# Backward of a spectral and dense block: where w2's gradient is scaled, and when the last stage's inputs are loaded

## The chip, the cores and the metric

One core of a Trainium2 chip runs the kernel in one launch. The metric is device time in microseconds of an execution, as the median of a set of runs. Engines are named PE (matmul), DVE (VectorE), ACT (ScalarE), POOL (GpSimd); the SP queue issues most DMAs.

## The reference

A block with six modulation rows, forward and all gradients but that of `B_x`:

```python
mod = (silu(c) @ w_mod).reshape(1, 6, 1, 512)
sa, ca, ga, sb, cb, gb = ...                       # its six rows
h = layernorm(x) * (1 + ca) + sa
x = x + ga * irfft2(rfft2(h) * (w_r + 1j * w_i))   # 2048 x 512
h = layernorm(x) * (1 + cb) + sb
x = x + gb * (relu(h @ w1 + b1) ** 2 @ w2 + b2)    # inner width 1792
out, vjp = jax.vjp(f, A_x, A_w_r, A_w_i, B_w1, B_b1, B_w2, B_b2, c, w_mod)
return out, *vjp(grad_out)
```

For what follows, three gradients matter. With g the output gradient (2048 x 512) and h the squared relu (2048 x 1792), w2's is h^T (g * gb), b2's is the column sum of g * gb, and that of `A_x` comes out of the last stage, the backward of the spectral mix and of the first layernorm.

## The kernel before, in words

Rows are kept as 16 tiles of 128 (NT = 16), inner features as 14 chunks of 128 (NFC = 14). All arrays are bf16, sums are fp32 in PSUM. The program is written with a tile framework: each tile comes from a named pool with a number of buffers, the framework adds the waits, and each engine and the SP queue then work through a fixed order. That order is chosen when the kernel is built, by program order (raised by `high_priority`) among what is ready. `tc.issue_after(ins)` puts what is traced inside it behind `ins` on that engine or queue. Pools lie on a stack on either side of SBUF, so a new pool may have to wait until the work on an old one's tiles has ended.

The parts up to some 290 us (forward, dense backward, the forward half of the spectral backward) are untouched. After them come:

1. `spec_f23` with `ew_b` and `after_b` (eight groups gi). For each group PE does the transforms L323 and L311, ACT copies out, DVE does the complex products (`cmul`, L418 to L421), which give Z in place and gW, the filter gradients; SP writes gW out (L1170; three buffers). `after_b` runs after each group: it loads later groups, puts in units of w1's gradient (`fill_w1`, L1126, 16 units of 16 matmuls, copied by ACT L1130, written out by POOL L1132), takes the products for the modulation rows (`gm.emit`: broadcast L463, copy L465, DVE L474 and L475, ACT L472, output by POOL L477), loads the transform LGb (L1177), the first two `hn` (h's chunk, transposed by DMA from `h_dram`, L1067) and at group 5 the whole output gradient `g_sb` (L1188, 2 MB).
2. `spec_g1` (L346, eight groups of two halves in four PSUM buffers). The halves are copied to CS in turn by DVE (L351) and ACT (L353); psF follows with L365 and L367.
3. The last stage, eight pairs of row tiles. `g2_pair` makes psT (L375) and ACT copies it to Tsb (L377); `row_pair` makes psY (L385), ACT copies it to gs (L1276), DVE unfolds it (L266 to L270), multiplies (L1278), ACT scales with a sum (L1280), then DVE has q1 (L1281, needs n1), jk (L1285), rr, gn, gs and gx (L1287 to L1292), and SP writes gx (L1293). n1 and gxl of a pair come from `load_rows3` (L1222, L1223, pool `fin` with two buffers, two pairs ahead). Column sums go to PE later (L1262).

Between these, `fill` puts in the three last units of w1's gradient and then the 14 units of `grad_w2` (L1203, 16 matmuls each, two PSUM buffers `mm`, copied by DVE with the multiplication by the gate row, L1206, written by SP, L1207). `grad_b2` (L1214, `add_quadrants`) comes once, and two more `gm.emit` at the end; the last instructions are the row for c's gradient, L1319 to L1326.

`load_hn` takes two buffers in `hnp`, then two in `gwp`, and from the point at which w1's gradient is complete four in a pool `endp`; up to four further loads (`endp["more"]`) are put in with the first units.

Of the kernel before, what the change touches and what calls it, by code (L numbers as in the profile page):

```python
# [18 lines left out]
D = 512  # L19
# [4 lines left out]
NT = 16  # L24
# [311 lines left out]
def spec_g1(tc, K, Z, CS):  # L336
    nc = tc.nc
    with tc.tile_pool(name="psG", bufs=4, space=PSUM) as psG_pool, tc.tile_pool(name="psF", bufs=1, space=PSUM) as psF_pool:
        psF = psF_pool.tile([P, 4, P], FP32, name="psF")
        for gi in range(8):  # L340
            for hh in range(2):
# [8 lines left out]
                if hh == 0:  # L350
                    nc.vector.tensor_copy(out=dst, in_=src)  # L351
                else:
                    nc.scalar.copy(out=dst, in_=src)  # L353

            if gi % 2 == 1:
                for ri in range(2):
                    for n in range(2 * gi - 2, 2 * gi + 2):
                        q = 32 * (n % 4)
                        nc.tensor.matmul(psF[q:q + 1, n // 4, :], lhsT=Z[n // 2][:, n % 2, ri, 256:257], rhs=K["LG"][:, n, ri + 1, :],
                                         start=(ri == 0), stop=(ri == 1), tile_position=(0, q))  # L360
        for i in range(4):
# [82 lines left out]
class GMod:  # L444
# [13 lines left out]
    def emit(self, jc, q, row, pool, ppool):  # L458
# [8 lines left out]
        for dc in range(0, 4, 2):  # L467
            wmc = self.tiles[jc][dc // 2]
            gwm = pool.tile([P, 2, D], BF16, name="gwm", bufs=2)
# [11 lines left out]
def kernel(  # L481
# [580 lines left out]
    def load_hn():  # L1062
        fc = len(hns)
        if fc < NFC:
            pool = hnp if fc < 2 else endp.get("hn", endp["gw"])
            hns.append(pool.tile([P, NT, P], BF16, name="hn", bufs=2 if pool is not endp.get("hn") else 4))
            nc.sync.dma_start(hns[fc], h_dram[fc, :, :], transpose=True)  # L1067

    lf2 = tc.alloc_tile_pool(name="lf2", bufs=1, side="right")
    gmp = tc.alloc_tile_pool(name="gmp", bufs=1, side="right")  # L1070
# [22 lines left out]
    def add_quadrants(ps, pool, out, scale=None):  # L1093
# [6 lines left out]
        def add():  # L1100
# [5 lines left out]
            if scale is not None:  # L1106
                nc.vector.tensor_tensor(row, row, scale, op=ALU.mult)
# [6 lines left out]
    def run_later(n=1):  # L1114
        if later:
            later[0][0] -= n
            if later[0][0] <= 0:
                later.pop(0)[1]()

# [29 lines left out]
    with tc.tile_pool(name="f23b", bufs=2) as fr, tc.tile_pool(name="ewb", bufs=2) as ew:  # L1149
# [22 lines left out]
        def after_b(gi):  # L1172
            if gi + 4 < 8:
                load(gi + 4)
            if gi == 3:
                with tc.issue_after(K["gW"]):
                    nc.sync.dma_start(K["LG"], LG_dram)  # L1177
            fill_w1(2 if 0 < gi < 6 else 1)
            if gi == 4:
                with tc.issue_after(K["gW"]):  # L1180
                    load_hn()
                    load_hn()
            if gi == 5:
# [3 lines left out]
                with tc.issue_after(K["gW"]):  # L1187
                    K["g_load"] = nc.sync.dma_start(endp["g_sb"], g_view).ins  # L1188
            if gi in (0, 1, 3, 4):
                gms.pop(0)[1]()  # L1190
                if len(gms) > 1:
                    gm.load(gms[1][0], gmp)
# [3 lines left out]
    fin = tc.alloc_tile_pool(name="fin", bufs=2, side="right")  # L1196
# [3 lines left out]
    def grad_w2(fc):  # L1200
        ps = mmps.tile([P, SB], FP32, name="mm")
# [3 lines left out]
        with tc.high_priority():  # L1205
            nc.vector.tensor_tensor(gw, ps, modb[:, GB_B, :], op=ALU.mult)  # L1206
        nc.sync.dma_start(out6_view[:, fc, :], gw)  # L1207
        load_hn()

    def grad_b2():  # L1210
# [4 lines left out]
        add_quadrants(ps, gwp, out_7[None, :], modb[0:1, GB_B, :])  # L1215

    rows3 = {}

    def load_rows3(t):
        if t < NT:  # L1220
            rows3[t] = (fin.tile([P, 2, D], BF16, name="n1"), fin.tile([P, 2, D], BF16, name="gxl"))
            nc.sync.dma_start(rows3[t][0], n1_dram[:, t:t + 2, :])  # L1222
            nc.sync.dma_start(rows3[t][1], gx1_dram[:, t:t + 2, :])  # L1223

    with tc.issue_after(K["g_load"]):
        load_rows3(0)
        load_rows3(2)
    for _ in range(2):
        load_hn()

    CS = utcs.tile([P, NT, 4, 16, 8], BF16, name="utcs")
    spec_g1(tc, K, Z, CS)
    sp.release()
    lg2.release()
    fp = tc.alloc_tile_pool(name="fin2", bufs=2, side="right")
    psX = tc.alloc_tile_pool(name="psX", bufs=1, space=PSUM)
    units2 = [lambda fc=fc: grad_w2(fc) for fc in range(NFC)]

    def fill(n):
        for _ in range(n):  # L1240
            if units:
                fill_w1(1)
                if not units:
# [3 lines left out]
                    endp["more"] = 4  # L1247
            elif units2:
                units2.pop(0)()
                run_later()  # L1250
                if endp.get("more", 0) > 0:
                    endp["more"] -= 1
                    load_hn()

    with tc.tile_pool(name="psE", bufs=2, space=PSUM) as psE, tc.tile_pool(name="psS1", bufs=1, space=PSUM) as psS1:
# [11 lines left out]
        def row_pair(t, Ts):  # L1267
# [26 lines left out]
            load_rows3(t + 4)  # L1294

        Ts = g2_pair(0)
        for t in range(0, NT, 2):
# [4 lines left out]
            if t == 10:  # L1302
                grad_b2()
        fill(1)
# [6 lines left out]
        for j in range(2):  # L1311
            gm.load(j, endp["gm"])
            gm.emit(j, 32 * j, acc1_sb[32 * j:32 * j + 1, :], endp["gm"], psX)
# [15 lines left out]
    gwp.release()  # L1329
    fin.release()  # L1330
    endp["g"].release()
# [40 lines left out]
```

## Time and profile before

| what | value |
|---|---|
| median of 10 runs | 431.06 us (430.0 to 555.48) |
| the profiled execution | 430.68 us |
| its span in the profile | 428.9 us |
| its mean granted PE clock | 0.996 |
| SP issues in the span: transposing loads of hn | 14, 2.0 to 5.7 us each on the queue, 4.5 to 6.7 us to landing |

The page gives the busy time of each engine over the span, and tables by window cut it into stages. A busy PE need not be PE at its peak. The time reported by the runs contains 1.8 us that lie outside the span.

### The profile page before, as it was taken

Reading aid. Unit: us, or ns where it says so; the run is one execution under the profiler, and the core shown is the slowest. Engines: PE = TensorE matmul, PEld = TensorE weight load, DVE = VectorE, ACT = ScalarE, POOL = GpSimd, SP = SyncE. Lnnn points to the kernel's source line nnn. Section 1 sums busy time; section 2 is a strip of 40 time slices with the busy share of each in tenths; the row PEclk is TensorE's granted clock in tenths of the full one; section 3 lists DMA queues with packets and bytes.
Section 4 is the critical chain, followed back from the end, with each engine's and each line's share of the span. In section 5 each row is a group of like instructions: output and inputs, shape, how many; then the busy total and the mean of one; then the engine's idle time right before and its main releaser. Section 6 shows DMA issues by size and latency. Waiting matters only on the chain.

```text
span 428.9 us, 7116 instructions
## 1 busy us (share of the span) xinstructions
PE 397.6 (93%) x2353; PEld 196.1 (46%) x2375; DVE 354.1 (83%) x862; ACT 256.2 (60%) x487; POOL 54.7 (13%) x135
## 2 busy tenths in 40 slices
PE   2789999999899999999999999999999999898995
PEld 0344446654434444444444444455555654343332
DVE  6799868959996588978897998937998945999994
ACT  5578699778882188248635855454756463536331
POOL 8347940000000000000000000002221000000011
PEclk9999999999999999999999999999999999999899
DMA  8999899969497469767965998988899999999993
GB/s 235 215 263 300 261 213 320 305 222 227 139 357 231 129 93 337 204 168 180 307 168 172 178 318 266 299 171 286 276 250 331 181 248 220 224 247 268 254 255 112
DMA packets 144227, 101.11 MB, mean 236 GB/s; under 512 B 98969, under 2 KB 127518, under 8 KB 143806
## 3 DMA queue, kind: packets, MB, share of 16 engines
q1 hardware_dynamic: 141034, 93.03, 83.3%
q0 software_dynamic: 2592, 7.09, 5.6%
q10 hardware_dynamic: 564, 0.53, 0.5%
q8 instruction: 19, 0.31, 0.3%
q14 instruction: 18, 0.15, 0.1%
HBM read 35.44 MB, written 41.60 MB: 180 GB/s over the span
## 4 chain that ended last, share of the span: by engine, by line
PE 50%; DVE 21%; ACT 15%; DMA 7%; issue 4%; POOL 1%; ACTq 0%; DVEq 0%; SPq 0%
PE og L906 12%; PE mm L877 10%; PE mm L1126 8%; PE mm L712 5%; PE mm L1203 3%; PE psG L346 2%; DMA out_dram<-gW 2%; ACT gab L717 2%; PE psC L311 2%; DVE jk L1285 2%; ACT AE L329 2%; DMA n<-n_dram 2%; DMA wmc<-in_w_mod_dram 1%; PE psB L323 1%; ACT AE L330 1%
## 5 line engine op out<-in xcount | busy, mean ns | idle before, releaser
L712 PE MATMUL mm<-gT,w2T 128*128 128x512 bf16 x224 | 57.8, 383 | 2.9 <-ACT gab L717 2.9
L877 PE MATMUL mm<-h2T,w 128*128 128x512 bf16 x224 | 53.4, 378 | 1.6 <-ACT r L879 1.4
L1203 PE MATMUL mm<-g_sb,hn 128*128 128x512 bf16 x217 | 51.7, 387 | 3.2 <-DVE gw L1206 2.6
L906 PE MATMUL og<-w1T,gab 128*128 128x512 bf16 x218 | 49.9, 379 | 1.0 <-DVE o L971 0.8
L1126 PE MATMUL mm<-gab,h_sb 128*128 128x448 bf16 x256 | 50.7, 352 | 0.0
L906 PE MATMUL og<-w,h 128*128 128x512 bf16 x217 | 49.1, 379 | 0.3
L879 ACT ACTIVATE r<-mm,b1col 128x512 bf16<-128x512 f32 x56 | 37.0, 685 | 6.1 <-PE mm L877 3.3
L1203 PEld LDWEIGHTS <-hn 128*128 128x128 bf16 x224 | 21.6, 100 | 30.0 <-issue 7.7
L877 PEld LDWEIGHTS <-w 128*128 128x128 bf16 x224 | 21.1, 97 | 30.0 <-issue 8.3
L1126 PEld LDWEIGHTS <-h_sb 128*128 128x128 bf16 x256 | 24.6, 98 | 21.8 <-issue 0.6
L906 PEld LDWEIGHTS <-h 128*128 128x128 bf16 x224 | 21.8, 98 | 26.1 <-issue 0.9
L906 PEld LDWEIGHTS <-gab 128*128 128x128 bf16 x224 | 21.6, 98 | 25.9 <-issue 1.4
L712 PEld LDWEIGHTS <-w2T 128*128 128x128 bf16 x224 | 21.2, 98 | 22.4 <-issue 6.3
L1280 ACT ACTIVATE gs<-gn,inv 128x512 bf16<-128x512 bf16 x16 | 11.4, 715 | 25.1 <-DVE gn L1278 25.1
L919 ACT CAST G<-og 128x512 bf16<-128x512 f32 x16 | 9.2, 580 | 28.1 <-PE og L906 28.1
L295 POOL MEMSET AE<- 128x2 bf16 x4 | 0.3, 102 | 194.2 <-DMA gx_dram<-n2rows 194.2
L477 POOL DMA_DIRECT2D out_dram<-gwm x12 | 8.7, 729 | 122.4 <-DMA hn<-h_dram 57.9
L881 DVE TENSOR_TENSOR h<-r 128x1024 bf16<-128x1024 bf16 x28 | 19.2, 685 | 4.8 <-ACT r L879 4.8
L717 ACT CAST gab<-mm 128x512 bf16<-128x512 f32 x36 | 21.3, 600 | 2.0 <-PE mm L712 1.8
L475 DVE SCALAR_TENSOR_TENSOR gm_junk<-wmc,onef,gmbc 128x512 bf16<-128x512 bf16 x24 | 17.9, 745 | 3.0 <-DMA wmc<-in_w_mod_dram 2.0
L715 DVE CAST gab<-mm 128x512 bf16<-128x512 f32 x20 | 13.8, 688 | 7.9 <-PE mm L712 7.7
L377 ACT ACTIVATE Tsb<-psT 128x512 bf16<-128x512 f32 x32 | 18.4, 607 | 1.6 <-PE psT L375 1.5
(290 smaller groups left out, 800.2 us busy)
## 6 DMA issues: line engine op xcount, KB each, us to landing
h_dram<-h SPq DMA_DIRECT2D x28, 256.0 KB, 3.2
gh_dram<-gab SPq DMA_DIRECT2D x28, 256.0 KB, 4.1
w<-in_B_w_dram SPq DMA_DIRECT2D x2, 1792.0 KB
wmc<-in_w_mod_dram SPq DMA_DIRECT2D x12, 256.0 KB, 5.7
out_dram<-gwm POOLq DMA_DIRECT2D x12, 256.0 KB, 6.4
wz_dram<-Z SPq DMA_DIRECT2D x8, 258.0 KB, 3.9
xs_dram<-Xs SPq DMA_DIRECT2D x8, 258.0 KB, 4.3
Z<-wz_dram SPq DMA_DIRECT2D x8, 258.0 KB, 5.5
```

The costliest lines, as they stand in the source:

```text
L377: nc.scalar.activation(Tsb, ps, AF.Copy, scale=EF_S)
L475: nc.vector.scalar_tensor_tensor(out=junk, in0=wmc[:, i, :], scalar=K["onef"], in1=gmbc, op0=ALU.mult, op1=ALU.mult, accum_out=self.gsc[:, ...
L712: nc.tensor.matmul(ps, lhsT=w2T[:, dc, fc * P:(fc + 1) * P], rhs=gT[b][:, :, dc, :], start=(dc == 0), stop=(dc == 3))
L715: nc.vector.tensor_copy(out=gaT[b][:, fc, :], in_=ps)
L717: nc.scalar.copy(out=gaT[b][:, fc, :], in_=ps)
L877: nc.tensor.matmul(ps, lhsT=w1[:, dc, (fc + i) * P:(fc + i + 1) * P], rhs=h2T[b][:, :, dc, :], start=(dc == 0), stop=(dc == 3))
L879: nc.scalar.activation(r[:, i, :], ps, AF.Relu, bias=b1col[:, fc + i:fc + i + 1])
L881: nc.vector.tensor_tensor(h2, r, r, op=ALU.mult)
L906: nc.tensor.matmul(ps, lhsT=lhs(fc), rhs=rhs[:, fc, :], start=(fc == 0), stop=(fc == NFC - 1))
L1126: nc.tensor.matmul(ps[:, 0:W4], lhsT=h2_sb[:, t, dc * P:(dc + 1) * P], rhs=ghn[t // 4][:, t % 4, fs], start=(t == 0), stop=(t == NT - 1))
L1203: nc.tensor.matmul(ps, lhsT=hns[fc][:, t, :], rhs=g_sb[:, t, :], start=(t == 0), stop=(t == NT - 1))
L1280: nc.scalar.activation(gs[:, i, :], gn[:, i, :], AF.Copy, scale=inv1[:, t + i:t + i + 1], accum_out=rr[:, i, 0:1])
```

## The change

- `grad_w2`'s copy out of PSUM is a plain copy by ACT; the gate row is multiplied into `g_sb` in SBUF before, in four DVE instructions of four row tiles each (`scale_g`, called from `spec_g1` after groups 4 to 7, each behind the DVE cast just issued). `grad_b2` then needs no scaling of its own.
- `fin` is allocated earlier, and `load_rows3(0)` and `(2)` follow LGb's load at group 3. Every third pair's rows have a buffer in `fp` (fin2), so loads run three pairs ahead.
- `g_sb` is loaded at group 4, in four pieces, after that group's `gm.emit`; the first two `hn` are issued behind it.
- `load_hn` is issued once at the start of each unit but the first, behind the row load named by `K["rows"]` or the one before it (`K["rows0"]`); the extra loads fall away.
- The last two `gm.load` are issued at t = 10, and the last `gm.emit` has four `gwm` buffers.

```diff
-def spec_g1(tc, K, Z, CS):
+def spec_g1(tc, K, Z, CS, after=None):
...
                 if hh == 0:
-                    nc.vector.tensor_copy(out=dst, in_=src)
+                    K["cast"] = nc.vector.tensor_copy(out=dst, in_=src).ins
...
+            if after:
+                after(gi)
...
-    def emit(self, jc, q, row, pool, ppool):
+    def emit(self, jc, q, row, pool, ppool, nbuf=2):
...
-            gwm = pool.tile([P, 2, D], BF16, name="gwm", bufs=2)
+            gwm = pool.tile([P, 2, D], BF16, name="gwm", bufs=nbuf)
...
-            nc.sync.dma_start(hns[fc], h_dram[fc, :, :], transpose=True)
+            with tc.issue_after(K["rows" if fc < 4 else "rows0"]):
+                nc.sync.dma_start(hns[fc], h_dram[fc, :, :], transpose=True)
...
+    fin = tc.alloc_tile_pool(name="fin", bufs=2, side="right")
     gmp = tc.alloc_tile_pool(name="gmp", bufs=1, side="right")
...
-            if scale is not None:
-                nc.vector.tensor_tensor(row, row, scale, op=ALU.mult)
...
+    def load_rows3(t):
+        if t < NT:
+            pool, n = (endp["fp"], 1) if t % 6 == 4 else (fin, 2)
+            rows3[t] = [pool.tile([P, 2, D], BF16, name=x, bufs=n) for x in ("n1", "gxl")]
+            nc.sync.dma_start(rows3[t][0], n1_dram[:, t:t + 2, :])
+            K["rows0"] = K.get("rows")
+            K["rows"] = nc.sync.dma_start(rows3[t][1], gx1_dram[:, t:t + 2, :]).ins
...
             if gi == 3:
                 with tc.issue_after(K["gW"]):
                     nc.sync.dma_start(K["LG"], LG_dram)
+                    load_rows3(0)
+                    load_rows3(2)
             fill_w1(2 if 0 < gi < 6 else 1)
+            if gi in (0, 1, 3, 4):
+                gms.pop(0)[1]()
+                if len(gms) > 1:
+                    gm.load(gms[1][0], gmp)
             if gi == 4:
-                with tc.issue_after(K["gW"]):
-                    load_hn()
-                    load_hn()
-            if gi == 5:
                 gmp.release()
...
                 with tc.issue_after(K["gW"]):
-                    K["g_load"] = nc.sync.dma_start(endp["g_sb"], g_view).ins
-            if gi in (0, 1, 3, 4):
-                gms.pop(0)[1]()
-                if len(gms) > 1:
-                    gm.load(gms[1][0], gmp)
+                    for t in range(0, NT, 4):
+                        K["g_load"] = nc.sync.dma_start(endp["g_sb"][:, t:t + 4, :], g_view[:, t:t + 4, :]).ins
+                with tc.issue_after(K["g_load"]):
+                    load_hn()
+                    load_hn()
...
     def grad_w2(fc):
+        if fc > 0:
+            load_hn()
...
-            nc.vector.tensor_tensor(gw, ps, modb[:, GB_B, :], op=ALU.mult)
+            nc.scalar.copy(out=gw, in_=ps)
         nc.sync.dma_start(out6_view[:, fc, :], gw)
-        load_hn()
...
-    with tc.issue_after(K["g_load"]):
-        load_rows3(0)
-        load_rows3(2)
-    for _ in range(2):
-        load_hn()
...
+    def scale_g(gi):
+        if gi >= 4:
+            gs = g_sb[:, 4 * gi - 16:4 * gi - 12, :]
+            with tc.issue_after(K["cast"]):
+                nc.vector.tensor_tensor(gs, gs, modb[:, GB_B, None, :].broadcast_to([P, 4, D]), op=ALU.mult)
+
+    spec_g1(tc, K, Z, CS, scale_g)
...
+    endp["fp"] = fp
+    load_rows3(4)
+    for _ in range(2):
+        load_hn()
...
-                    endp["more"] = 4
...
-                if endp.get("more", 0) > 0:
-                    endp["more"] -= 1
-                    load_hn()
...
-            load_rows3(t + 4)
+            load_rows3(t + 6)
...
             if t == 10:
                 grad_b2()
+                with tc.issue_after(K["rows"]):
+                    gm.load(0, endp["gm"])
+                    gm.load(1, endp["gm"])
...
-            gm.load(j, endp["gm"])
-            gm.emit(j, 32 * j, acc1_sb[32 * j:32 * j + 1, :], endp["gm"], psX)
+            gm.emit(j, 32 * j, acc1_sb[32 * j:32 * j + 1, :], endp["gm"], psX, 4)
```

## Prediction before the run

> **What bounds the kernel now.** I read the page's busy shares first, then a table of ten-microsecond windows over the last part of the kernel, then the waits of that part, then the timelines of TensorE (PE), VectorE (DVE) and the SP queue around each wait, and the chain last. Columns of a window row: stretch, its length, busy us and instruction count of PE, PEld, DVE, ACT, POOL, granted clock, DMA share, GB/s.
>
> ```profile
> PE 397.6 (93%) x2353; PEld 196.1 (46%) x2375; DVE 354.1 (83%) x862; ACT 256.2 (60%) x487; POOL 54.7 (13%) x135
> ```
>
> ```profile
> 350.00:360.00 10.00, 9.95 (x62) 5.27 (x61) 4.17 (x9) 6.44 (x15) 1.08 (x2) 1.00 1.03 197
> 360.00:370.00 10.00, 8.01 (x45) 3.66 (x45) 9.42 (x25) 3.45 (x8) 0.00 (x0) 1.00 1.11 229
> ...
> 390.00:400.00 10.00, 8.03 (x42) 3.22 (x42) 9.87 (x26) 4.43 (x11) 0.00 (x0) 0.91 1.02 237
> 400.00:410.00 10.00, 9.35 (x44) 3.50 (x43) 10.00 (x22) 5.16 (x12) 0.00 (x0) 0.92 1.00 240
> ```
>
> PE is the bound nearly everywhere, and is busy 9.7 or more of each ten us from 290 to 360. The exception is 360 to 410: there DVE is full, ACT is less than half busy, and PE has holes. Summed over the windows from 360 to 420 PE is idle 1.99 + 0.13 + 0.28 + 1.97 + 0.65 + 0.16 = 5.2 us. The PE timeline and the waits show where the holes are:
>
> ```profile
> 361.71 3.62 PE L1203 MATMUL mm<-g_sb,hn 128*128 128x512 bf16 x16
> 367.26 3.61 PE L1203 MATMUL mm<-g_sb,hn 128*128 128x512 bf16 x15 [1.93 <-DVE gw L1206]
> ...
> 396.90 0.86 PE L385 MATMUL psY<-Tsb,TAT 128*128 128x512 bf16 x2 [1.64 <-ACT Tsb L377]
> ```
>
> ```profile
> ACT gs L1280 <- DVE gn L1278: 25.1, 7, 6.1
> DVE q L1281 <- DMA n<-n_dram: 4.6, 1, 4.6
> PE mm L1203 <- DVE gw L1206: 2.6, 3, 1.9
> ```
>
> The first unit of w2's gradient leaves PE at 360.4, but its copy L1206 runs on DVE only at 366.52, because DVE had stood 4.62 us for the first n1 rows and the copy's place in its order is behind them. The second hole is the same cause one engine on: ACT's Tsb stands behind an activation that waits for DVE's gn. The n1 rows are late because of the SP queue: their issue waits for output packets lying behind the one 2 MB g_sb load, as the chain shows.
>
> ```profile
> 342.04 9.38 DMA out_dram<-gW
> 351.43 6.49 DMA n<-n_dram
> 357.94 0.69 DVE q L1281
> ```
>
> One more loss follows the second hole, in the two-microsecond windows:
>
> ```profile
> 398.00:400.00 2.00, 1.78 (x8) 0.72 (x6) 2.00 (x6) 0.00 (x0) 0.00 (x0) 0.54 0.92 291
> 400.00:402.00 2.00, 2.00 (x7) 0.80 (x6) 2.00 (x4) 0.85 (x2) 0.00 (x0) 0.61 1.01 217
> ```
>
> The granted clock falls to 0.54 and 0.61 for 4 us: 2 x 0.46 + 2 x 0.39 = 1.7 us of PE work lost. Recoverable in this stretch: 5.2 + 1.7 = 6.9 us.
>
> **The change, part by part.** The sums are against the profiled execution, 430.68 us (span 428.9 and 1.8 around it); the median shown, 431.06, lies 0.4 above it.
>
> *Copies of w2's gradient from DVE to ACT.* DVE loses 14 L1206, which occupy it 0.60 us each start to start (684 ns busy): 8.4 us, and the 0.4 us multiply L1107. The nearest ACT row, L717, is 600 ns for the same 128x512 out of PSUM: 8.4 us more for ACT, which is at 3.5 to 6.4 us per ten here, so its time is hidden in idle time. The Trainium skill speaks against this step: "ScalarE: Activation LUTs", section "Rules for kernel authors", sends multiplications and other simple elementwise work to VectorE, said to be up to about three times faster per element in bf16. By that rule a copy on ACT might take up to 2 us and 14 of them 28 us, which ACT hasn't got. But the source here is fp32 in PSUM, and the same cast stands on both engines in this trace: 688 ns on DVE (L715), 600 on ACT (L717). I take the row. The real risk is order: behind the copy on ACT's queue stand Tsb and gs, and the copy may itself stand behind an L1280 that waits for gn (25.1 us in 7 such waits). If every copy fell behind one, the 6.9 us would not come back; if none, none is lost. Since DVE is freed of 1.1 us per pair of rows and of the n1 wait, I expect short waits and take 0.5 us.
>
> What DVE then needs: the gx instructions at 370.46 and 408.76 are five pairs apart, 7.66 us each, with nine L1206 between; without them (7.66 - 9 x 0.60 / 5) 6.6. PE's own work between the psY at 370.71 and at 396.90 is 26.2 less 1.9 idle over four pairs, 6.1 each. DVE is still slower by 0.5 per pair, 3.5 over seven pairs, but each tile of a pair has two buffers, so PE may run some two pairs (13 us) ahead. DVE stops being the bound.
>
> *Scaling g_sb.* Four new DVE multiplies of 128x2048. L1278 and L266 give 0.60 us for 1024 elements and 0.34 for 512, so 0.53 per further 1024: about 1.15 each, 4.6 us. They stand between the L351 casts of CS in spec_g1, after groups 4 to 7. From the first such cast (341.72) four casts of 0.61 and four multiplies fill DVE to 348.7; then come the four copies of psF, DVE and ACT in turn, which took from 345.32 to 348.00. CS is whole at 351.4 instead of 348.0, so g2's first psT can start 3.4 us later. PE covers this if it runs the remaining 48 matmuls of w1's gradient first (32 take 6.05 us, so 9.1 us, from 345.2 to 354.3); they do run at 345 to 356 anyway. Without that cover PE stands up to 3.4 us. The program order is fixed before it runs and accounts for the multiplies in some way; I take 0.5 us.
>
> *Rows of pairs 0 and 1 loaded from group 3 on, pair 2 into its own buffer.* Four SP issues of about 0.4 us move from 351-355 to just behind LGb at 322. The 4.6 us wait for n1 goes. Late next on DVE is CS itself, by the 3.4 us just found: q of pair 0 moves only from 357.9 to about 356.7. The move puts 1 MB in front of the outputs gW of group 4. At the 360 to 380 GB/s moved in 328-332 that is 2.8 us. gW has three buffers, so group 7's gW on DVE (338.05) waits for those outputs; they are issued at 322.6-329.4 and take 7 to 12 us to land, some 334-337 now, 337-340 then. Between 0 and 2 us of wait, with the CS casts queued behind it and PE behind these (it already waits 0.3 us at 339.45): I take 1.0. LGb itself is issued first; it landed 11.5 us after 321.93, at 333.4, against its use at 336.5: 3 us to spare.
>
> *g_sb in four pieces from group 4 on, the first two hn behind it.* g_sb takes the place of the gmod buffers, whose last output is issued on POOL at 324.89 and takes 6 to 10 us, 331 to 335. The SP queue is held for it, with hn 0 and 1 and the later gW behind. Then 2 MB at some 270 GB/s: pieces landing from about 340 to 347. DVE wants them at 342.3, 344.1, 345.8 and 347.6. That is tight: 0 to 3 us late, each DVE microsecond going into CS; PE's w1 matmuls may hide it. I take 0.5. hn 0 then lands near 350 and is used at 357: hidden; were it 7 us later, PE would stop.
>
> *hn one by one.* Load k+3 is issued at the start of unit k and behind an earlier row load. The SP queue spends 2.0 to 5.7 us on each, and it lands 4.5 to 6.7 us after issue. Three units of 3.45 us cover that. But hn 4 stands behind the rows of pair 4, which need gx of pair 1 (about 368): it lands near 375, used at about 375 to 377; hn 7 is as close. Cost 0 to 3 us, I take 0.5. The four wmc loads move from 380-383 to after 388, used after 404: hidden. Four gwm buffers instead of two remove ACT's 1.0 us wait, off the path; POOL's issues stay in order.
>
> Sum: -6.9 + 0.5 + 0.5 + 1.0 + 0.5 + 0.5 = -3.9 us, 426.8 for such an execution, 427.2 with the 0.4 to the median; I say 427.0. The end (last copy, gcr, its output, 4.5 us after PE's last unit) is unchanged. Unknowns run from -6.9 (423.8) to about -1 (430).
>
> **The clock rule.** "TensorE: Matmul & The Clock Gate", Part 1, has the clock fall to half only after a whole idle window of about 3.4 us. Here PE was never idle longer than 1.64 us (2.25 us busy in 394-398) and the clock still fell. By the rule nothing but the 5.2 us idle could be got back (about -2.2 net, 428.8) and a new short stop would be free of it; by the row a gap of 1.6 us can cost 1.7 more. The row decides, for the gain and for the rival below. The gap at 365 did not cost it, so it is no certainty.
>
> **Rivals.**
> 1. *Group stage starves (slower).* Mechanism: g_sb's last piece lands at 350 or later, three or more us behind its place, because rows and LGb lie before it in SP's order. DVE, in order, holds the CS casts; CS is whole at 354; psT stands in PE's order before the covering matmuls. PE loses 3 to 6 there, 2 for the gW buffers, 1.7 clock: 7 to 10 against 6.9 gained. It decides from 6.9 us of new PE idle on. For it: the DMA share is 1.15 in 330-340, and in 336-338, with two transposes under way, the rate falls to 117 GB/s. Against: the transposes now come behind g_sb, and 9.1 us of PE work are at hand. It gives about 433.5; chance 0.22.
> 2. *ACT takes DVE's place (partly or no gain).* Copies behind L1280 stop PE as L1206 did: 3 to 5 of the 6.9 remain lost and the front costs 2: 429 to 432; chance 0.13. Against: the priority given to the copy and ACT's idle 4 to 6 us per pair.
> 3. *hn is late.* PE waits 1 to 3 us in two or three units: 428 to 430; chance 0.10.
> The main forecast, 423.8 to 428.5, has 0.55.
>
> **Numbers.** This kernel's measurement can tell about 0.3%, 1.3 us. Faster (below 429.8): 0.55, all of 3 but a little, and a third of rival 2: 0.69. Same: 0.08. Slower: 0.23. Range 423.0 to 433.2.
>
> **What would show it.** Right: no n1 wait on DVE near 354; L1206's place on ACT within 1 us of PE's unit end; PE over 9.7 in each window of 360-410 and clock 1.00; DVE near 8.5 there; g2's first psT at 348 to 352 with PE idle under 1 us before it. Wrong: PE waiting for DVE utcs in 338-346 or for CS near 350 by more than 3 us; PE waiting for hn; or ACT's copies 3 us or more after their units.

## The result, and the profile after

The changed kernel takes 438.8 us (median of 11 runs, 436.02 to 443.68), the kernel before beside it 430.05: ratio 1.0206, 95% interval [1.0175, 1.0237]. It is slower by about 9 us, on the other side of the forecast of 427.0. The profiled execution took 437.38 us, its span is 435.6. Lines have moved by two to fifteen, the rows' loads further: psT L377, Tsb L379, psY L387, hn L1070, gW out L1182, g_sb's load L1203, w2's matmuls L1218, their ACT copy L1221, n1 L1128, the multiplication of g_sb L1237. In the kernels of the experiments they differ again by a few; the names of the tiles in a row say which instruction it is.

First the busy shares on the page of the changed kernel:

```profile
PE 397.8 (91%) x2353; PEld 196.2 (45%) x2375; DVE 350.4 (80%) x851; ACT 264.5 (61%) x501; POOL 54.7 (13%) x135
```

Then its table of ten-microsecond windows (columns as in the prediction: stretch, length, busy us and count of PE, PEld, DVE, ACT, POOL, granted clock, DMA share, GB/s):

```profile
350.00:360.00 10.00, 4.53 (x30) 2.49 (x28) 0.71 (x2) 3.23 (x7) 0.50 (x1) 0.91 0.43 99
360.00:370.00 10.00, 9.95 (x62) 5.09 (x61) 7.64 (x19) 6.65 (x15) 0.54 (x1) 0.92 0.79 186
...
380.00:390.00 10.00, 7.05 (x48) 2.97 (x48) 9.37 (x22) 5.36 (x13) 0.00 (x0) 1.00 0.96 222
390.00:400.00 10.00, 9.95 (x64) 4.64 (x64) 7.98 (x18) 5.74 (x15) 0.00 (x0) 1.00 1.07 232
400.00:410.00 10.00, 7.72 (x40) 3.15 (x39) 9.71 (x26) 5.87 (x15) 0.00 (x0) 1.00 1.06 278
```

PE's work is the same (397.8 us, 397.6 before). It stands 5.5 us in 350 to 360, where before it stood 0.05, loses another 1.7 to the clock (0.91 and 0.92 over ten us each), and stands 5.2 in 380 to 390 and 400 to 410 together, where before it stood 0.9. PE's timeline in the changed kernel (start, duration, engine, line, operation, and in brackets the idle time before it and what ended it) says for what:

```profile
358.57 0.59 PE L387 MATMUL psY<-Tsb,TAT 128*128 128x512 bf16 x1 [5.33 <-ACT Tsb L379]
...
385.06 3.40 PE L1218 MATMUL mm<-g_sb,hn 128*128 128x512 bf16 x15 [0.77 <-DMA hn<-h_dram]
389.85 3.63 PE L1218 MATMUL mm<-g_sb,hn 128*128 128x512 bf16 x16 [1.39 <-DMA hn<-h_dram]
...
410.36 0.82 PE L1218 MATMUL mm<-g_sb,hn 128*128 128x512 bf16 x3 [2.48 <-DMA hn<-h_dram]
...
427.58 3.63 PE L1218 MATMUL mm<-g_sb,hn 128*128 128x512 bf16 x15 [0.69 <-DMA hn<-h_dram]
```

There are two holes of different origin: 5.33 us before the first psY, and four late hn, 5.3 us together. ACT's timeline leads the first one further back, in the same columns:

```profile
351.44 0.58 ACT L369 CAST utcs<-psF 1x512 bf16<-1x512 f32 x1 [0.75 <-DVE utcs L367]
357.93 1.09 ACT L379 ACTIVATE Tsb<-psT 128x512 bf16<-128x512 f32 x2 [5.91 <-DMA out_dram<-gW]
```

CS is whole at 352.02 (351.44 + 0.58), psT follows within a microsecond, and then Tsb waits 5.91 us for an *output*, the filter gradient gW, which has nothing to do with it. The SP queue's timeline (start, time on the queue) shows when these outputs and the hn go out:

```profile
333.36 3.75 SPq L1203 DMA_DIRECT2D g_sb<-in_grad_out_dram  x4
337.15 8.09 SPq L1070 DMA_TRANSPOSE hn<-h_dram  x2
345.35 8.73 SPq L1182 DMA_DIRECT2D out_dram<-gW  x12
357.79 0.35 SPq L1128 DMA_DIRECT2D n<-n_dram  x1
...
358.66 5.98 SPq L1070 DMA_TRANSPOSE hn<-h_dram  x2
...
379.57 0.33 SPq L1128 DMA_DIRECT2D n<-n_dram  x1
379.99 2.77 SPq L1070 DMA_TRANSPOSE hn<-h_dram  x1
...
383.90 3.31 SPq L1070 DMA_TRANSPOSE hn<-h_dram  x1
```

The last twelve gW leave at 345 to 354, behind the two transposing loads, and land near 358. And the fifth hn is issued only at 379.99, behind row loads that wait for DVE to free their buffers.

Why Tsb waits for gW is seen in the addresses of the built program (bytes in each partition). The first tiles of the pool fin2 are Tsb and, new in the changed kernel, the rows of pair 2. The pool is laid over pools already released:

```
              fin2               ewb (p1 from 130112, gW from 138432)
before        96704 to 129920    not touched
after         96704 to 134016    overlapped by fin2
```

The change puts a row buffer (n1 and gxl, 4 KB) into fin2 and moves b2's three tiles out of gwp, so fin2 now ends inside ewb. The built programs show what follows. Before the change, the values that the first Tsb waits for are reached by loads (Z, Xb, LGb); in the changed kernel they are reached by the outputs of the last two gW, though Tsb's own bytes (100800 to 102848) touch none of ewb and fin2 as a whole ends below gW. So the framework lets the first work in a new pool wait for all work on every pool under it. The load of pair 2's rows at 357.79 waits in the same way, for 3.5 us by SP's table of waits, and with it the queue and the two hn behind.

### The profile page after: what moved, and what is told of

Same layout as the page of the kernel before. It is cut to its first block, busy times and chain, and to the rows that moved or that the text cites. A ratio compares the mean times of both kernels' runs of the same rounds, so it can differ in the third digit from the quotient of the medians.

```text
span 435.6 us, 7129 instructions
## 1 busy us (share of the span) xinstructions
PE 397.8 (91%) x2353; PEld 196.2 (45%) x2375; DVE 350.4 (80%) x851; ACT 264.5 (61%) x501; POOL 54.7 (13%) x135
## 4 chain that ended last, share of the span: by engine, by line
PE 41%; DVE 21%; DMA 16%; ACT 14%; issue 4%; SPq 2%; POOL 1%; ACTq 0%; DVEq 0%
PE og L908 10%; PE mm L879 8%; PE mm L714 6%; PE mm L1218 5%; DMA hn<-h_dram 5%; DMA out_dram<-gW 4%; PE psG L346 2%; DMA LGb<-LG_dram 2%; ACT gab L719 2%; ACT AE L329 2%; SPq L1182 2%; DMA h_dram<-h 1%; ACT Xs L313 1%; DMA wmc<-in_w_mod_dram 1%; DMA y<-gx_dram 1%
## 5 line engine op out<-in xcount | busy, mean ns | idle before, releaser
L1218 PE MATMUL mm<-g_sb,hn 128*128 128x512 bf16 x217 | 50.2, 379 | 5.9 <-DMA hn<-h_dram 5.3
L1218 PEld LDWEIGHTS <-hn 128*128 128x128 bf16 x224 | 20.9, 98 | 31.9 <-DMA hn<-h_dram 6.9
L379 ACT ACTIVATE Tsb<-psT 128x512 bf16<-128x512 f32 x32 | 18.5, 604 | 7.4 <-DMA out_dram<-gW 5.9
L1142 ACT CAST gw<-mm 128x448 bf16<-128x448 f32 x16 | 8.7, 541 | 22.3 <-PE mm L1138 22.3
```

Of the source, the lines that this page charges most:

```text
L379: nc.scalar.activation(Tsb, ps, AF.Copy, scale=EF_S)
L1218: nc.tensor.matmul(ps, lhsT=hns[fc][:, t, :], rhs=g_sb[:, t, :], start=(t == 0), stop=(t == NT - 1))
```

## The experiments

All ratios are against the kernel before, measured beside each run on the same chip; its median there was 427.6 to 428.8 us. My theory was that the overlap of fin2 and ewb makes the hole at 353, and hn issued behind row loads the other losses. The edits are to the changed kernel where nothing else is said.

### Address and hn order, each alone and both

e1_addr puts b2's tiles back and moves two late tiles out of fin2; the order of instructions on PE, DVE, ACT and SP stays as it was.

```diff
-        add_quadrants(ps, endp["gm"], out_7[None, :])
+        add_quadrants(ps, gwp, out_7[None, :])
...
-        acc1_odd = fp.tile([64, D], FP32, name="acc1_odd", bufs=1)
+        acc1_odd = endp["gm"].tile([64, D], FP32, name="acc1_odd", bufs=1)
...
-        acc1_sb = fp.tile([64, D], BF16, name="acc1_sb", bufs=1)
+        acc1_sb = endp["gm"].tile([64, D], BF16, name="acc1_sb", bufs=1)
```

> The changed kernel with the same instructions in the same order on every engine and queue; only addresses differ: b2's three small tiles lie in gwp again and acc1's two tiles in endp, so that pool fin2 ends below the pool ewb that holds gW. Theory P (pool overlap: the first tile of fin2 waits for all work on the pool ewb under it, the last gW outputs included): Tsb starts within 1 us of its psT near 352 instead of 357.9, the 5.3 us PE hole and the half clock behind it (1.7) go, time 6 to 8 us below the changed kernel, 430 to 433. Rival H (late hn loads set the end, PE would wait there instead): time within 2 us of the changed kernel's, 437 to 439, with longer PE waits for hn. Rival Q (the SP queue, not the address, holds Tsb): the 5.9 us wait stays.

Measured: 430.66 us, 1.0058 [1.0038, 1.0078]. Its PE timeline has no wait at the first psY; late hn are still there:

```profile
377.30 3.40 PE L1218 MATMUL mm<-g_sb,hn 128*128 128x512 bf16 x15 [0.51 <-DMA hn<-h_dram]
382.19 3.63 PE L1218 MATMUL mm<-g_sb,hn 128*128 128x512 bf16 x16 [1.49 <-DMA hn<-h_dram]
...
403.36 1.23 PE L1218 MATMUL mm<-g_sb,hn 128*128 128x512 bf16 x3 [3.14 <-DMA hn<-h_dram]
```

So 1.5 of the 2.06% was an address, with no instruction moved: in the built programs the order on every engine is the same.

e6_hn_only undoes only the loading of hn.

```diff
-            with tc.issue_after(K["rows" if fc < 4 else "rows0"]):
-                nc.sync.dma_start(hns[fc], h_dram[fc, :, :], transpose=True)
+            nc.sync.dma_start(hns[fc], h_dram[fc, :, :], transpose=True)
...
-        if fc > 0:
-            load_hn()
...
         nc.sync.dma_start(out6_view[:, fc, :], gw)
+        load_hn()
...
                     endp["hn"] = endp["gm"] = tc.alloc_tile_pool(name="endp", bufs=2)
+                    endp["more"] = 4
...
                 units2.pop(0)()
                 run_later()
+                if endp.get("more", 0) > 0:
+                    endp["more"] -= 1
+                    load_hn()
```

> The changed kernel with only the hn loads put back as before; fin2 still lies over ewb. If the two costs add: the 5.3 us hole near 353 stays and the hn waits go, 3 to 6 us below the changed kernel, 432 to 436. If the pool hole alone makes the hn loads late (everything on SP is shifted with it), the time stays at 437 to 439.

Measured: 432.18 us, 1.0084 [1.0062, 1.0106]. No wait for hn is left, and the hole is (PE's timeline):

```profile
357.71 0.59 PE L387 MATMUL psY<-Tsb,TAT 128*128 128x512 bf16 x1 [5.08 <-ACT Tsb L379]
```

e5_addr_hn has both edits.

> The kernel of the address experiment (e1) with the hn loads as they were before the change: one behind each unit's output, four more with the first units, tied to no row load. Theory H (what is left of the slow-down in e1 is PE waiting 5.1 us for hn, which stands on SP behind row loads that wait for DVE): the hn waits go, the half clock at 400 too, 4 to 6 us below e1: 424 to 427 where e1 is 430.7. Rival L (DVE's last pair sets the end: PE waits for the column sums of the last pair instead): only 1 to 3 us below e1, 428 to 430, with PE waits for gh or q near 400 instead of hn.

Measured: 427.89 us, 0.9985 [0.9962, 1.0007]. Only one wait for hn is left (0.42 us near the end), so both causes are the ones supposed. But the time is 2.8 us below e1 and not 4 to 6, since PE now stands elsewhere (below). The four ratios give the size of each, from its value with the other still there to its value alone:

```
                       hn as changed   hn as before   worth of hn
address as changed        1.0206          1.0084         1.2%
address as before         1.0058          0.9985         0.7%
worth of the address       1.5%            1.0%
```

But what is left once both are undone can't be told from no change: where 3.9 us net were forecast (0.9%, out of 6.9 recoverable), the interval allows 0.4% at the most.

### Two tests of the address

e2_hn_behind_gW leaves fin2 over ewb, and moves the first two hn behind gW of the last group, so that these outputs go out early.

```diff
-                with tc.issue_after(K["g_load"]):
-                    load_hn()
-                    load_hn()
...
             fill_w1(2 if 0 < gi < 6 else 1)
+            if gi == 7:
+                with tc.issue_after(K["gW"]):
+                    load_hn()
+                    load_hn()
```

> The changed kernel with the first two hn loads issued behind the gW outputs of group 7 instead of behind g_sb at group 4; fin2 still lies over ewb. Theory P: the wait for the last gW output stays but ends 8 us earlier (the two transposes no longer stand before them on SP), so Tsb waits under 1 us and the time falls 5 to 7 us below the changed kernel, 431 to 434. Theory A (address alone, outputs late for another reason): Tsb still starts near 358, time 437 to 439. If hn 0 then comes late for its first unit at 364 it costs back what it is late.

Measured: 431.73 us, 1.0065 [1.0033, 1.0097]. The hole at the first psY is gone as with the other address: the overlap costs only while the outputs beneath are late, here behind the 8.09 us that two transposing loads hold the queue. PE's waits for hn are 6.5 us.

e7_before_b2_moved is the kernel *before* with b2's tiles in the later pool, and nothing else of the change.

```diff
-        add_quadrants(ps, gwp, out_7[None, :], modb[0:1, GB_B, :])
+        add_quadrants(ps, endp["gm"], out_7[None, :], modb[0:1, GB_B, :])
```

> The kernel before with b2's three small tiles moved from gwp to endp, nothing else: gwp shrinks by 4 KB, so fin2, which lies under it, ends 4 KB higher and reaches over ewb. Theory P: the first Tsb now waits for the gW outputs of group 7, which before the change land near 352 to 357: PE stands 3 to 8 us near 350, 4 to 9 us above before, 432 to 437. If the address costs only with the new order on SP: within 1.5 us of before.

Measured: 434.9 us, 1.0135 [1.0084, 1.0186]. Its PE timeline at the first psY, and ACT's:

```profile
356.18 0.58 PE L385 MATMUL psY<-Tsb,TAT 128*128 128x512 bf16 x1 [6.94 <-ACT Tsb L377]
```

```profile
355.53 1.08 ACT L377 ACTIVATE Tsb<-psT 128x512 bf16<-128x512 f32 x2 [7.52 <-DMA gxl<-gx_dram]
```

The trace puts the wait down to a load of gxl, which is the transfer that ended last on one of the counters that SP's transfers share. In the built program the values that Tsb waits for are those that the outputs of the last two gW reach, as in the changed kernel.

Moving three small tiles from one pool to another makes the kernel before 1.35% slower (four runs, 0.8 to 1.9%), some 5.8 us, with nothing else of the change in it.

### Where the expected gain went: parts put alone into the kernel before

e3_act_copy_only: w2's gradient is copied by ACT, and the gate is left out of it, so DVE has neither L1206 nor the multiplications of g_sb.

```diff
-            nc.vector.tensor_tensor(gw, ps, modb[:, GB_B, :], op=ALU.mult)
+            nc.scalar.copy(out=gw, in_=ps)
```

> The kernel before with one edit: w2's copy out of PSUM is a plain copy on ACT; the multiplication by the gate row is left out of w2's gradient. This measures the step of the prediction alone, without the cost of scaling g_sb. Prediction's step: DVE loses 8.4 us, the copies do not wait for DVE, the PE holes of 1.9 and 1.6 us and the half clock go: 3 to 6 us below before, 424 to 427. Rival (copies stand behind L1280 on ACT, which waits for gn): within 1.5 us of before, PE waits for ACT gw instead.

Measured: 429.46 us, 1.0023 [0.9997, 1.0049]. PE is busy 9.95 of each ten us from 350 to 390, as forecast, and does not wait for ACT's copies, as the rival had it. But then it stands at two places of its timeline (0.70 and 1.17 us there in e9, the second profile of the kernel before, below):

```profile
395.01 0.86 PE L385 MATMUL psY<-Tsb,TAT 128*128 128x512 bf16 x2 [1.25 <-ACT Tsb L377]
...
404.67 0.38 PE L1262 MATMUL acc<-gh,ones_q 128*32 128x512 bf16 x1 [2.75 <-DVE gh L270]
```

e4_rows_early_only: rows of pairs 0 and 1 are loaded behind LGb at group 3.

```diff
+    fin = tc.alloc_tile_pool(name="fin", bufs=2, side="right")
...
                     nc.sync.dma_start(K["LG"], LG_dram)
+                    load_rows3(0)
+                    load_rows3(2)
...
-    with tc.issue_after(K["g_load"]):
-        load_rows3(0)
-        load_rows3(2)
```

> The kernel before with one edit: pool fin is allocated early and the rows of pairs 0 and 1 are loaded behind LGb at group 3. Prediction's step: DVE's 4.6 us wait for n1 goes, the first PE hole (1.9 us at 365) goes, nothing else moves: 2 to 4 us below before, 426 to 428. Rival (the megabyte in front of group 4's gW stops group 7's gW on DVE and then spec_g1): PE idle of 1 to 2 us near 339, time within 1 us of before or above.

Measured: 427.86 us, 0.9985 [0.9964, 1.0005]: the same picture, full until 390, then 1.64 us for Tsb at 394.44 and 1.18 for gh at 403.25.

e9_before_again is the kernel before, profiled again.

> The kernel before, with nothing changed, as a yardstick: the earlier ratios stand between two kernels, while the 6.9 us of the prediction were added up in one profiled execution of 430.7 us, and on this chip the kernel before has a median near 428.3. Theory R (the holes are a fixed property of the program): the ratio is 1.000 within 0.003, the first n1 rows are waited for by 4 to 5 us, PE is idle again by about 5.2 us between 360 and 420, and the clock is halved for some 4 us once. Rival S (part of the 6.9 us is chance): PE's idle time there is below 4 us or the clock is not halved, and then a kernel without these holes has correspondingly less to win than was reckoned.

Measured: 428.23 us, 1.0004 [0.9983, 1.0024], profiled execution 427.68. Its table of waits, DVE from 330 to 400 (total, times, longest):

```profile
DVE q L1281 <- DMA n<-n_dram: 0.8, 1, 0.8
```

Its windows of the stretch:

```profile
360.00:370.00 10.00, 9.95 (x63) 4.67 (x63) 9.25 (x21) 4.89 (x13) 0.00 (x0) 1.00 1.12 208
...
390.00:400.00 10.00, 8.80 (x42) 3.46 (x42) 9.87 (x24) 5.95 (x14) 0.00 (x0) 1.00 0.99 211
400.00:410.00 10.00, 7.70 (x36) 2.82 (x35) 9.30 (x24) 4.55 (x9) 0.00 (x0) 1.00 1.03 229
```

And its PE timeline where PE still stands:

```profile
393.04 0.86 PE L385 MATMUL psY<-Tsb,TAT 128*128 128x512 bf16 x2 [0.70 <-ACT Tsb L377]
...
401.86 0.38 PE L1262 MATMUL acc<-gh,ones_q 128*32 128x512 bf16 x1 [1.17 <-DVE gh L270]
```

This is theory S. The 4.62 us wait for n1, on which the forecast stood, is 0.8 here; the clock is never halved; PE stands 3.7 us from 360 to 420 (0.05 three times, 1.20, 2.30, 0.05) instead of losing 6.9. The two executions run alike up to the first psY (349.17 and 349.12); PE's last matmul is at 423.64 in the one and at 420.39 in the other. Those 3.25 us are about the difference 6.9 - 3.7. Nearly half of what was counted as recoverable is thus not there in a second profile of the same kernel. (Whether the late n1 belonged to one execution or to the first set of runs, nine of whose ten lie between 430.0 and 432.8, two profiles can't say.) What is left, at 390 to 410, is the same hole that e3 and e4 end in.

### What makes the hole at 390 to 410

After both repairs (e5) PE stands up to 394.21 for the last pair's Tsb, 1.55 us, and the clock costs 1.7 around it (0.83 over ten us). Its PE timeline and its windows:

```profile
394.21 0.86 PE L387 MATMUL psY<-Tsb,TAT 128*128 128x512 bf16 x2 [1.55 <-ACT Tsb L379]
```

```profile
390.00:400.00 10.00, 8.34 (x33) 3.10 (x32) 9.13 (x23) 7.12 (x16) 0.00 (x0) 0.83 1.04 216
```

From 360 to 420 PE loses 2.24 us of standing and 1.7 of clock, 3.9 in all, against 3.7 in the kernel before. That fits the ratio of 0.9985.

e8_addr_hn_sums_later is e5 with two more units of w2 ahead of the last column sums.

```diff
-        fill(1)
+        fill(3)
         late.flush()
```

> The kernel e5 with the column sums of the last pairs put behind two more units of w2's gradient (fill(3) ahead of late.flush()). Theory L (the last pair on DVE stops PE at these four small matmuls in PE's order): 1 to 3 us below e5. If PE does not wait for them in e5, or the modulation rows behind them come late: equal to e5 or 1 to 3 us above.

Measured: 430.2 us, 1.0032 [1.001, 1.0055], 2.3 us above e5: the second case. In e5 PE's table of waits has none for the column sums, so there was nothing to win; and PE now waits 1.84 us for Tsb, 2.58 for a copy of w2's unit, and 1.50 at the end for c's gradient, which comes later with the sums.

e10_order_both and e11_order_tsb are e5 with ACT's order changed: in the pair loop (pool psE) Tsb goes ahead of gs, in e10 the copies of psY too.

```diff
-    nc.scalar.activation(Tsb, ps, AF.Copy, scale=EF_S)
+    (nc.scalar.activation(Tsb, ps, AF.Copy, scale=EF_S) if pool.name != "psE" else ahead(tc, nc.scalar.activation, Tsb, ps, AF.Copy, scale=EF_S))
...
+def ahead(tc, f, *a, **k):
+    with tc.high_priority(): f(*a, **k)
...
-                nc.scalar.copy(out=gs[:, i, :], in_=psY)
+                with tc.high_priority(): nc.scalar.copy(out=gs[:, i, :], in_=psY)
```

> The change with its addresses and its hn loads put back (0.9985 before), and in the pair loop ACT's copies of psY and its Tsb take precedence over gs. Theory A (the hole left at 394 is made by ACT's order: Tsb of the last pair and the copies of psY stand behind a gs that waits 3 us for DVE's gn): PE's wait of 1.55 us for Tsb near 394 falls below 0.3, the half clock after it (1.7 us) goes too, and the time falls by 2 to 3 us against 427.9: ratio 0.991 to 0.995. Theory B (DVE's seven pairs at 7.3 us each set the end, whatever ACT's order): PE stops a little later instead, at the column sums of the last pairs that wait for DVE's gh (L270) or q, by 1.5 to 3 us near 400 to 408, and the ratio stays at 0.997 to 1.001.

> As the run with both, but only Tsb takes precedence over gs, the copies of psY stay where they were. Theory A with Tsb as the only cause: as good as with both, 0.991 to 0.995. If the buffers of psY count as well (the last pair's psY needs the pair before it copied out first, at 393.6), the wait at 394 becomes one for ACT's gs copies, still 1 us or more, and the ratio is 0.996 to 0.999. Theory B: 0.997 to 1.001 with the wait at the column sums.

Measured: 427.46 us, 0.9994 [0.9975, 1.0013], and 428.48, 1.0006 [0.9985, 1.0027]. Neither gains. PE no longer waits for Tsb there, but 2.69 us (e10) and 2.75 (e11) for the psY buffers that ACT empties. That is where the last expectation put the wait if these buffers count; the ratios are those of theory B, whose place for it, the column sums, is not seen. The PE timeline of e10, then ACT's:

```profile
396.44 1.04 PE L387 MATMUL psY<-Tsb,TAT 128*128 128x512 bf16 x2 [2.69 <-ACT gs L1285]
```

```profile
395.80 1.07 ACT L1285 CAST gs<-psY 128x512 bf16<-128x512 f32 x2 [2.36 <-DVE gx L1301]
```

ACT's copy in its turn waits for DVE's gx of a pair before, which frees the gs buffer that the copy writes.

e12_rows_early_order_both gives e4 the same two edits.

> The kernel before with its rows of pairs 0 and 1 loaded early (0.9985 alone) and ACT's copies of psY and Tsb ahead of gs; w2's gradient is still copied out and scaled on DVE, g_sb and hn are as before. Theory A: the wait near 394 goes and the ratio is 0.992 to 0.996. Theory B: DVE is 9.8 of 10 busy here from 390 to 410, more than in the changed kernel, so the wait comes back at the column sums, 0.997 to 1.001, and this version is no better than, and by up to 1 us worse than, the one with the copies on ACT.

Measured: 429.89 us, 1.0049 [1.0029, 1.0068], worse by more than theory B allowed; PE waits 1.76 us for gh at 404.31, and the clock is 0.83 from 400 to 410.

So putting these instructions ahead on ACT doesn't release the pairs. Two causes were left: DVE's pairs start late in e5 (the multiplications of g_sb delay CS, first psY 352.66 instead of 349.12), or DVE and ACT hold each other.

e14_no_scaling is e5 without the four multiplications.

```diff
-            with tc.issue_after(K["cast"]):
-                nc.vector.tensor_tensor(gs, gs, modb[:, GB_B, None, :].broadcast_to([P, 4, D]), op=ALU.mult)
+            pass
```

> The change with its addresses and its hn loads put back (0.9985), and without the four multiplications of g_sb (the gate is left out of w2's gradient). Theory C (they make CS whole 3.6 us later: first psY at 352.7 against 349.1; PE is covered there, but DVE's eight pairs start 4 us later, and DVE is what PE waits for at 390 to 404): first psY near 349, last gx near 404 instead of 409, no PE wait over 0.5 us from 390 to 404, no half clock there, ratio 0.989 to 0.993. Rival D (the pairs are held by ACT and DVE waiting for each other, not by the start): the hole near 394 stays at 1 us or more, ratio 0.996 to 0.999.

Measured: 427.67 us, 0.9981 [0.9963, 1.0]. Theory C falls: the first psY is at 349.27, yet the last gx comes at 409.69 and not near 404, and PE stands 2.76 us, now at the column sums, in its timeline:

```profile
402.64 0.58 PE L1271 MATMUL acc<-gh,ones_q 128*32 128x512 bf16 x1 [2.76 <-DVE gh L270]
```

What DVE waited for from 340 to 412 (total, times, longest):

```profile
DVE jk L1294 <- ACT gs L1289: 3.2, 9, 0.4
```

And ACT in the same stretch:

```profile
ACT gs L1289 <- DVE gn L1287: 18.2, 8, 3.7
```

DVE's timeline in e14 shows how it comes to wait in each pair:

```profile
374.00 0.69 DVE L1287 TENSOR_TENSOR gn<-gh,modb 128x1024 bf16<-128x1024 bf16 x1
374.61 0.69 DVE L1290 TENSOR_TENSOR q<-gh,n 128x1024 bf16<-128x1024 bf16 x1
375.64 0.75 DVE L1294 SCALAR_TENSOR_TENSOR jk<-gs,onef,n 128x512 bf16<-128x512 bf16 x1 [0.34 <-ACT gs L1289]
```

And the same place in the kernel before, from DVE's timeline in e9:

```profile
389.84 0.69 DVE L1281 TENSOR_TENSOR q<-gh,n 128x1024 bf16<-128x1024 bf16 x1
390.44 0.68 DVE L1098 TENSOR_TENSOR b4l<-mm,b 128x512 bf16<-128x512 f32 x1
391.04 0.68 DVE L1206 TENSOR_TENSOR gw<-mm,modb 128x512 bf16<-128x512 f32 x1
391.64 0.74 DVE L1285 SCALAR_TENSOR_TENSOR jk<-gs,onef,n 128x512 bf16<-128x512 bf16 x1
```

gn goes to ACT, gs comes back for jk, and q is all that DVE has in between. With the copies, one of them stands in that gap and DVE does not wait; without them DVE waits. From the first gx to the seventh the kernel before takes (405.50 - 358.04) / 6 = 7.91 us a pair, e14 (401.24 - 357.73) / 6 = 7.25. Ten copies of 0.60 us lie in the former and none in the latter, so by the prediction's way of counting 6.9 was to be expected: 0.34 a pair, 2.1 us over six, came back, most of it as waits for ACT's gs (2.5 us in e14 against 1.0 in e9). And gh of the last pair, for which PE waits, is behind the seventh gx in e14's order (whole at 402.59), while in the kernel before it stands ahead of it (401.81): DVE is 4.3 us earlier with the seventh gx and later with the one tile that PE needs. The ratio is rival D's, and its mutual wait is in the trace; the place is not, since the hole near 394 shrank to 0.48 us and a larger one opened at the sums. How much each of the two, the mutual wait and the order of the last unfold, is worth was not tried apart.

e15_scale_on_pool is e5 with the multiplications on POOL.

```diff
-                nc.vector.tensor_tensor(gs, gs, modb[:, GB_B, None, :].broadcast_to([P, 4, D]), op=ALU.mult)
+                nc.gpsimd.tensor_tensor(gs, gs, modb[:, GB_B, None, :].broadcast_to([P, 4, D]), op=ALU.mult)
```

> As the run without multiplications, but they are done on POOL, which has nothing from 342 to 357. If POOL takes up to 3 us for each (the multiplication of 128x2048 takes DVE 1.21), the last piece is ready by 355, ahead of the first unit at 356, and theory C gives 0.989 to 0.994 here too; rival D 0.996 to 1.000. If POOL takes 5 us or more, or slows DVE's casts beside it, PE waits at the first units by more than 3 us and the ratio is above 1.003.

Measured: 431.69 us, 1.006 [1.0033, 1.0087]. Three multiplications take 13.47 us, 4.5 each:

```profile
337.98 13.47 POOL L1235 TENSOR_TENSOR g_sb<-g_sb,modb 128x2048 bf16<-128x2048 bf16 x3 [9.58 <-DMA g_sb<-in_grad_out_dram]
```

The last is ready at 356.1, yet PE's first unit of w2 starts 2.57 us late at 360.37, and gh is again late by 2.76 at 407.44. DVE's timeline, then ACT's, show what stood in the way:

```profile
351.73 4.65 DVE L266 TENSOR_TENSOR unf_u<-gs 128x512 bf16<-128x512 bf16 x1 [3.66 <-ACT gs L1285]
```

```profile
358.33 0.72 ACT L1289 ACTIVATE gs<-gn,inv 128x512 bf16<-128x512 bf16 x1 [5.64 <-DVE gn L1287]
```

An unfold that takes DVE 0.42 us elsewhere ends only when POOL's last multiplication (352.01 to 356.09) has ended. ACT then waits 5.64 us for gn, and behind that, at 359.76, stand its copies of w1's last units, which free the PSUM buffers for PE's unit. So e15 is not the same experiment as e14 on another engine: POOL held DVE up for 4.2 us, and theory C is tested by e14 alone.

e13_after_again is the changed kernel beside the others.

> The changed kernel, nothing altered, as a yardstick beside the runs above. Theory (the two costs found, address and hn order, are all of the loss): 1.0058 - 0.9985 and 1.0084 - 0.9985 add to 1.7%, so 1.016; with the overlap of a hole and a late load 1.015 to 1.022. Rival (something else is in it that shows only in its first measurement, 1.0206): below 1.012. The hole before psY near 357 (5 us, waiting for Tsb) and 4 to 6 us of waits for hn are there again, or it was chance.

Measured: 438.68 us, 1.0214 [1.0165, 1.0263]: the loss is as in the first measurement, with a hole of 3.99 us before the first psY and 5.2 us of waits for hn. Alone the two costs add to 1.7%; that the other 0.4% comes of their meeting fits the table of four and is within the widths of its intervals.

## Why the prediction was wrong

The forecast was -3.9 us and the measurement is +9. Two terms of the sum failed on the way down, g_sb's place on SP, costed at nothing, and "hn one by one", costed at 0.5; and the 6.9 they were set against was for the most part not to be had.

- *The later gW behind g_sb and hn* is the step that was costed at nothing. The prediction follows instructions, queues and buffers, and reckons nowhere with the place of fin2; it says of g_sb's load "The SP queue is held for it, with hn 0 and 1 and the later gW behind" and adds no cost for it. The later gW did become late, and through the overlap Tsb was behind them: 5.3 us and 1.7 of clock. By the table of four, 1.0 to 1.5%.
- *hn one by one*, "0 to 3 us, I take 0.5": 5.3 us measured, and 0.7 to 1.2% of the time by the table of four. The mechanism (hn 4 behind rows that wait for gx) was named. The size was not: hn 4 was taken to land near 375 and was issued at 379.99, since the whole row chain had slid by the first hole, and each transposing load holds the queue (1.7 to 6.0 us in the changed kernel). In e1, without that slide, hn 4 is issued at 372.48 and PE still waits 5.1 us in all, so the order is enough by itself.
- *"Recoverable in this stretch: 6.9 us"* was the sum of one execution's holes. 3.2 of it are gone in a second profile in which n1 is late by 0.8 and not 4.6, and 3.7 are there without that. So the second hole is not "the same cause one engine on": in e4, with the rows loaded early and no first hole, it is 1.64 us as before.
- *"DVE stops being the bound"*, 7.66 less the copies gives 6.6 a pair: without copies it is 7.25 (e14) and 7.34 (e3), because a copy filled the time in which DVE waits for ACT. The buffers of two pairs that were to let PE run ahead hold until 390 and no longer.
- *The clock*: the prediction let the row decide that a 1.6 us gap can cost 1.7 us. It did in e5 (1.55), not in e4 (1.64), so "no certainty" was right and as a part of the gain it should have been counted at part of its size.
- *Right*: g_sb's multiplications (1.13 us start to start, DVE 1.15 forecast), CS whole at 352.0 (351.4 forecast) with PE at work to 353.2, no wait for g_sb, no wait for n1. Three rows of the changed kernel's DVE timeline show the pattern of casts and multiplications:

```profile
343.02 1.21 DVE L1237 TENSOR_TENSOR g_sb<-g_sb,modb 128x2048 bf16<-128x2048 bf16 x1
344.15 0.68 DVE L351 CAST utcs<-psG 128x512 bf16<-128x512 f32 x1
344.75 1.21 DVE L1237 TENSOR_TENSOR g_sb<-g_sb,modb 128x2048 bf16<-128x2048 bf16 x1
```

- The copies on ACT cost 0.56 to 0.59 us each, as the row said and not the 2 us that the prediction made of the rule on elementwise work, and PE waits for one only once, 0.15 us. The 1.0 for gW's buffers was not seen (PE waits 0.29 for the CS casts, 0.3 before).
- *Rival 1* had the sign and nearly the place, a group stage whose late transfers stop PE ahead of the first psY, but by g_sb, which was on time; its own terms give 430.8 to 433.8, and "about 433.5" is their upper end. *Rival 3*, and with it the sign "PE waiting for hn", was true and larger than written: 5.3 us in four units. *Rival 2* was not seen.
- *"The end is unchanged"*: from PE's last matmul to the end of the span it is 3.5 us in e5 and e14 (421.43 to 424.9, 421.98 to 425.5) against 5.3 and 5.5 before, a gain of about 1.9 that was not foreseen. PE's last matmul is 1.0 us later in e5 than in e9, which leaves 0.9 in these two profiles; the medians of e5 have 0.6, less than their interval can tell from nothing.

No version here beats the kernel before by more than its measurement can tell: e14, which leaves work out, has 0.9981, e4 and e5 0.9985.

## What to carry to other kernels

When tiles change pools, list the pools' addresses and ask what the first tile of each new pool will lie over and which transfers out of it are still under way: three small tiles moved cost some 5.8 us with no instruction changed. Before a hole is counted as recoverable, profile the same kernel a second time: a hole made by the arrival of a transfer may be one execution's. And work taken off a full engine gives back only what is not already standing in its waits: look at what is beside it in the order, and which single tile the bound engine is waiting for.

## What the runs showed of the hardware that was not expected

- The granted clock fell to 0.83 over ten us, a loss of 1.7 us, after PE stops of 1.55 (e5), 1.76 (e12), 2.57 (e15), 2.75 (e3), 2.76 (e14) and 3.14 us (e1), and did not after stops of 1.64 (e4), 1.84 and 2.58 (e8), 2.48 (changed kernel) and 2.76 us (e15, the later one). In e3 and e12 it is 0.50 and then 0.64 or 0.65 in two windows of 2 us: (0.50 + 0.36) x 2 = 1.7 us, or some 3.4 us at half speed. "TensorE: Matmul & The Clock Gate", Part 1, in the Trainium skill, has a window of about 3.4 us, running freely of the kernel, and that would account for this length and for a stop of 2.76 us that counts in one run and not in another. By its rule only a wholly idle window halves the clock; here a stop of 1.55 us did, less than half of one, and the measurement stands. Where the stops lay in such a window no trace here shows, so what decides stays open.
- The same bf16 multiplication of 128x2048 takes POOL 4.5 us and DVE 1.21. Beside POOL's last one a DVE addition of two bf16 tiles in SBUF took 4.65 us in place of 0.42 (e15), while the DVE casts from PSUM beside the first ones kept their 0.69.
